# Softmax factors applied in the float16 split instead of in place, in an attention + two-layer kernel

## The chip, the cores and the metric

The kernel runs on one core of one Trainium2 chip. The metric is device time in microseconds (us) for one execution. Its engines are named as the profile names them: PE is TensorE (matrix products), PEld its weight loads, DVE is VectorE, ACT is ScalarE, POOL is GpSimd, and SP is SyncE, which here only issues DMAs. Each engine works through its own list of instructions in order, so an instruction that waits also holds up everything behind it on that engine.

## The reference

For 4 batches, 12 heads, 448 tokens and 64 numbers per head:

```
scores = cap * tanh((q @ k.T / sqrt(64)) / cap)          # cap = 30
p      = exp(scores - max(scores))
attn   = p / (sum(p) + 1e-9)
x      = heads of (attn @ v) side by side                # 1792 x 768
h      = x @ w_in                                        # 1792 x 2048
g      = max(h, 0) + alpha * min(h, 0)
out    = g @ w_out                                       # 1792 x 768, float32
```

## The kernel before

**Number format.** Most products run in float16 with float32 accuracy: an operand is split into a high part (its value rounded to float16) and a low part (the value minus the high part, again float16), and three products (high-high, high-low, low-high) are summed.

**Attention of batches 1 to 3.** The work is cut into 18 units (3 batches, 6 pairs of heads). A unit has 896 rows of scores (2 heads, 448 tokens), in 7 blocks of 128 rows and 448 keys; `steps` takes them two at a time. Per step: PE computes the scores into PSUM (L713), ACT writes their tanh into one of three buffers `tall` (L501), DVE takes each row's maximum (L506), POOL or DVE turns it into a bias (L508), ACT takes the exponential in place and sums each row (L513), DVE turns the sums into factors `rr`, which are 1/sum times 2^15 (L518, L520). Then, per block:

1. DVE multiplies the block in place by its factors (L522, recorded at L376, the line of the helper `scaled`).
2. ACT or DVE rounds it to float16: the high part, in one of three buffers `pw` (L536, recorded at L368 on ACT, L370 on DVE).
3. POOL or DVE subtracts: the low part (L537, recorded at L379, the helper `minus`).
4. SP issues one or two transposing DMAs from `pw` to `ptall` (L540), from which PE multiplies with the split `v` (L585); the result leaves PSUM by `xout` as another split pair, `xring`.

**Batch 0** works in float32 (`turn_32`: PE transposes the block, no split) except its last unit, of 4 blocks, which takes the way above with `gall` in the place of `tall`. So 126 + 4 = 130 blocks go through `turn_split`.

**The two layers.** `mm1` (L730) multiplies `xring` with `wi` and is evacuated by ACT or DVE (L374, L376), DVE (L740) and a split of `gr` into `gall` (high L368 or L370, low L379 on POOL or DVE). `mm2` (L771) multiplies `gall` with the split `w_out`. The weights arrive as 64-bit numbers and are converted and split by DVE, ACT and POOL (L826 to L841, L869 to L874). `mm1` of a batch needs all six units of its attention; `mm2` needs `mm1` of all its inner slices. While PE works on the attention of a batch, `mm1` and `mm2` of the batch before fill the rest of its time.

**The order** is written by a planner, `Plan`: each operation is given a priority and the engines that may do it with an expected time in ns, and a list scheduler gives the next ready operation to each free engine. Where an operation may go to ACT or DVE, its priority on DVE is worse by `PEN` = 114.44, and where to POOL or DVE, by `PEN2` = 133.12, so that DVE takes it only when it has little else ready. The expected times decide the order and the engine; the chip then runs the lists with semaphores.

Helpers that the change uses and that are there already:

```
scaled(e, o, i, s):      ACT: activation Copy with scale=s;  DVE: tensor_scalar o = i * s
split_lo(o, i, s, hi):   DVE: scalar_tensor_tensor o = (i * s) - hi
minus(e, o, a, b):       POOL or DVE: tensor_tensor o = a - b
```

`split_lo` is recorded at L382 and is used before for the splits of `q`, `k`, half of `v`, `xring` and part of the weights.

Of the kernel before, what the change touches and what calls it, by code (L numbers as in the profile page):

```python
# [75 lines left out]
class Plan:  # L76
# [15 lines left out]
    def op(self, prio, times, fn, r=(), w=(), rows=1.0):  # L92
        o = lambda: None
        o.prio, o.times, o.fn, o.rows, o.idx = prio, times, fn, rows, len(self.ops)
        o.handles, deps = [], set()
        for write, regions in ((False, r), (True, w)):
            for x in regions:
                if isinstance(x, Handle):
                    if x not in o.handles:
                        o.handles.append(x)  # L100
                        x.ops.append(o)
                    x = (x, 0, 1)
                space, lo, hi = x
                old = self.acc.setdefault(space, [])
                deps.update(e[2] for e in old if e[0] < hi and lo < e[1] and (write or e[3]))
                if write:
                    old[:] = [e for e in old if e[0] < lo or hi < e[1]]
        for write, regions in ((False, r), (True, w)):
            for x in regions:
                space, lo, hi = (x, 0, 1) if isinstance(x, Handle) else x  # L110
                self.acc[space].append((lo, hi, o.idx, write))
        o.deps = len(deps)
        o.next = []
        for d in deps:
            self.ops[d].next.append(o)
        self.ops.append(o)
        return o
# [114 lines left out]
def kernel(  # L232
# [89 lines left out]
    op = plan.op  # L322

    def chain(prio, fns, r=(), w=()):

        for fn in fns:
            op(prio, {"dve": 80}, lambda e, fn=fn: fn(), r=r, w=w)
# [38 lines left out]
    def copy(e, o, i):  # L366
        if e == "act":
            nc.scalar.activation(out=o, in_=i, func=AF.Copy)  # L368
        else:
            nc.vector.tensor_copy(o, i)  # L370

    def scaled(e, o, i, s):
        if e == "act":
            nc.scalar.activation(out=o, in_=i, func=AF.Copy, scale=s)  # L374
        else:
            nc.vector.tensor_scalar(out=o, in0=i, scalar1=s, scalar2=None, op0=ALU.mult)  # L376

    def minus(e, o, a, b):
        (nc.gpsimd if e == "pool" else nc.vector).tensor_tensor(out=o, in0=a, in1=b, op=ALU.subtract)  # L379

    def split_lo(o, i, s, hi):
        nc.vector.scalar_tensor_tensor(out=o, in0=i, scalar=s, in1=hi, op0=ALU.mult, op1=ALU.subtract)  # L382

    def either(n, psum=False):

        return {"act": 50 + 0.95 * n, "dve": 100 + (1.05 if psum else 0.55) * n}
# [63 lines left out]
    def spans(n, c):  # L450

        o = c * P
        for h in range(2):
            a, z = max(o, h * n), min(o + P, (h + 1) * n)
            if a < z:
                yield h, slice(a - o, z - o), slice(a - h * n, z - h * n)
# [11 lines left out]
    def t0_slot(i):  # L468

        if i % 5 < 4:  # L470
            a = i % 5 * 8
            lo = PART[1][0]
            return (gt[:, a:a + 8].rearrange("p (c j) k -> p c j k", j=NCH),
                    [(("g", r // 2), r % 2 * GW + lo, r % 2 * GW + lo + 2 * CP) for r in range(a, a + 8)])
        return pt32[:, -2 * S:].rearrange("p (c j k) -> p c j k", c=2, j=NCH), [("pt", 10 * S, 12 * S)]

    def steps(u, prio, n, S_, s_ns, sr_, scale, dma):

        nb = 2 * n // P
        u.sums = sums[:, u.idx % 3, :nb]  # L480
        for i0 in range(0, nb, 2):
            blocks = range(i0, min(i0 + 2, nb))
            m = len(blocks)
            i = step_no[0]
            step_no[0] += 1
            s = ps_s[i % 2]
            sr = (("S", i % 2), 0, 1)
            pr = prio + (ST1_P if u.b else ST_P) * i0

            def prods(e, blocks=blocks, s=s):  # L490
                for x, c in enumerate(blocks):
                    S_(s[:, x, :S], c)

            op(pr, {"pe": sum(s_ns(c) for c in blocks)}, prods, r=sr_, w=[sr])
            if u.b == 0:
                t, tr = t0_slot(i)
            else:
                t = tall[:, i % 3].rearrange("p c (j k) -> p c j k", j=NCH)
                tr = [("tall", i % 3 * 2 * S, (i % 3 + 1) * 2 * S)]
            t = t[:, :m]  # L500
            op(pr, {"act": 90 + 400 * m}, lambda e, s=s, t=t, m=m: nc.scalar.activation(  # L501
                out=t, in_=s[:, :m, :S].rearrange("p c (j k) -> p c j k", j=NCH), func=AF.Tanh, scale=scale[0]),
               r=[sr] + scale[1:], w=tr)
            mt = mxs[:, i % 6, :m]
            mr = (("m", i % 6), 0, 1)
            op(pr, {"dve": 20 + 490 * m}, lambda e, mt=mt, t=t: nc.vector.tensor_reduce(  # L506
                out=mt, in_=t, axis=AX.XY, op=ALU.max), r=tr, w=[mr])
            op(pr, {"dve": 130, "pool": 290}, lambda e, mt=mt: (nc.gpsimd if e == "pool" else nc.vector).tensor_scalar(  # L508
                out=mt, in0=mt, scalar1=ncap, scalar2=EXP_BIAS, op0=ALU.mult, op1=ALU.add), w=[mr])

            def exp(e, blocks=blocks, t=t, mt=mt):
                for x, c in enumerate(blocks):
                    nc.scalar.activation(out=t[:, x], in_=t[:, x], func=AF.Exp, scale=capt,  # L513
                                         bias=mt[:, x:x + 1], accum_out=u.sums[:, c:c + 1])

            op(pr, {"act": 735 * m}, exp, r=[mr], w=tr + [(("sums", u.idx % 3), c, c + 1) for c in blocks])
            r, rt = rr[:, u.idx % 3, i0:i0 + m], (("r", u.idx % 3), i0, i0 + m)
            chain(pr, (lambda r=r, su=u.sums[:, i0:i0 + m]: nc.vector.tensor_scalar(  # L518
                           out=r, in0=su, scalar1=GUARD, scalar2=1 / P_TOP if dma else 1.0, op0=ALU.add, op1=ALU.mult),
                       lambda r=r: nc.vector.reciprocal(out=r, in_=r)), r=[(("sums", u.idx % 3), i0, i0 + m)], w=[rt])  # L520
            for x, c in enumerate(blocks):
                op(pr, {"dve": 370}, lambda e, x=x, t=t, r=r: scaled(e, t[:, x], t[:, x], r[:, x:x + 1]), r=[rt], w=tr)  # L522
                if dma:
                    turn_split(u, pr, n, c, t[:, x], tr)
                else:
                    turn_32(u, pr, c, t[:, x], tr)

    blk_no = [0]

    def turn_split(u, pr, n, c, t, tr):  # L530

        w = pws[blk_no[0] % PW]
        wt = [(("pw", blk_no[0] % PW), z, z + 1) for z in range(2)]
        blk_no[0] += 1
        hi, lo = w[:, :NCH, :CP], w[:, NCH:, :CP]
        op(pr, {"act": 480, "dve": 310}, lambda e: copy(e, hi, t), r=tr, w=[wt[0]])  # L536
        op(pr, {"pool": 990, "dve": 540}, lambda e: minus(e, lo, t, hi), r=tr + [wt[0]], w=[wt[1]])  # L537
        for h, rows, cols in spans(n, c):
            full = rows.stop - rows.start == P
            op(pr, {"sp": (1294, 1275, 896) if full else (1225, 1275, 448)}, lambda e, h=h, rows=rows, cols=cols: nc.sync.dma_start_transpose(  # L540
                out=u.pt[h][:, :, cols], in_=w[rows].rearrange("p g k -> p (g k)")),
               r=wt, w=[("pt", u.po[h] + 4 * cols.start, u.po[h] + 4 * cols.stop)])

    def turn_32(u, pr, c, t, tr):

        h = plan.handle("a")

        def turn_P(e):
            for j in range(NCH):
                nc.tensor.transpose(ps_p[h.slot][:CP, j * P:(j + 1) * P], t[:, j], ident)  # L550

        ptw = ("pt", u.po[0] + c * P * NCH, u.po[0] + (c + 1) * P * NCH)
        op(pr, {"pe": 450}, turn_P, r=tr + [identr], w=[h, ptw])
        op(pr, either(512, True), lambda e: copy(
            e, u.pt[:, :, c * P:(c + 1) * P], ps_p[h.slot][:CP].rearrange("p (j t) -> p j t", j=NCH)), r=[h], w=[ptw])
# [64 lines left out]
    def attention32(part, pair):  # L620
# [30 lines left out]
        else:  # L651
            u.po = [po]
            u.pt = pt32[:CP, po:po + 8 * n].rearrange("p (j t) -> p j t", j=NCH)
        steps(u, prio, n, lambda s, c: nc.tensor.matmul(s, qz[:, c * P:(c + 1) * P], kt[:, pair], start=True, stop=True),  # L654
              lambda c: 750, [qr, ktr], [icap], dma)
        vt, vr = v0[0, pair]
# [371 lines left out]
```

## Time and profile before

| | |
|---|---|
| runs | 819.29, 820.54, 824.73 us; median 820.54 us |
| the profiled execution | 819.82 us; span from first to last instruction 818.0 us |
| PE | 712.3 us busy (87%), 4532 instructions |
| PEld | 419.5 us (51%) |
| DVE | 594.4 us (73%), 1250 instructions |
| ACT | 440.8 us (54%), 867 instructions |
| POOL | 313.1 us (38%), 307 instructions |
| mean granted TensorE clock | 0.949 |

Busy shares are averages over the whole span. The three stages differ: float32 attention and conversion of `w_in` up to about 160 us; attention of batch 1 with the conversion of `w_out` to about 300 us; attention of batches 1 to 3 beside `mm1` and `mm2` to about 660 us; then `mm2` and `mm1` alone.

### The profile page before, as it was taken

How to read it: one execution, taken by the hardware profiler on the slowest of the kernel's cores; microseconds unless marked ns; L12 is line 12 of the kernel's file. 1: busy time of each engine (PE TensorE's matmuls, PEld its weight loads, DVE VectorE, ACT ScalarE, POOL GpSimd, SP SyncE). 2: the span in 40 equal slices, each digit the busy share in tenths (PEclk: the TensorE clock that was granted, in tenths of full speed). 3: DMA queues.
4: the chain of work that ended last, by engine and by line, in shares of the span. 5: the costliest groups of instructions: out<-in, count | busy, mean ns of one | idle time of the engine just before them, and what ended most of it. 6: DMA issues, size and time to landing. Idle time of an engine off the chain costs nothing. (4 is left out here: it accounts for less than half of the span.)

```text
span 818.0 us, 12734 instructions
## 1 busy us (share of the span) xinstructions
PE 712.3 (87%) x4532; PEld 419.5 (51%) x4532; DVE 594.4 (73%) x1250; ACT 440.8 (54%) x867; POOL 313.1 (38%) x307
## 2 busy tenths in 40 slices
PE   8987877998678588947998998998899899999997
PEld 5655544676565244523444554554445455555664
DVE  3799997999999995797999976699889600344000
ACT  2767765887556673465765665476767400332000
POOL 1468563579675541333454522144454300000000
PEclk9999977999999599988999999999999999999999
DMA  9963422568646448877778867799876500000001
GB/s 212 274 202 119 156 77 89 164 119 169 164 133 129 90 80 165 157 171 152 126 128 152 152 129 162 138 192 161 161 147 114 100 20 20 20 1 1 20 20 38
DMA packets 227935, 98.62 MB, mean 121 GB/s; under 512 B 191456, under 2 KB 224160, under 8 KB 227872
## 3 DMA queue, kind: packets, MB, share of 16 engines
q1 hardware_dynamic: 227872, 97.82, 55.8%
q8 instruction: 35, 0.57, 0.3%
q14 instruction: 28, 0.23, 0.1%
HBM read 45.82 MB, written 5.51 MB: 63 GB/s over the span
## 5 line engine op out<-in xcount | busy, mean ns | idle before, releaser
L730 PE MATMUL p<-xring,wi 128*128 128x448 f16 (+2 forms) x1440 | 232.2, 320 | 8.9 <-DVE gr L740 8.0
L771 PE MATMUL p<-wp,gall 128*128 128x384 f16 x1344 | 230.2, 332 | 10.0 <-DVE gr L740 2.8
L730 PEld LDWEIGHTS <-wi 128*128 128x128 f16 x1440 | 138.0, 99 | 96.0 <-issue 14.5
L771 PEld LDWEIGHTS <-gall 128*128 128x128 f16 x1344 | 132.3, 99 | 102.6 <-issue 19.7
L379 POOL TENSOR_TENSOR pw<-tall,pw 128x448 f16<-128x448 f32 x100 | 115.6, 1160 | 118.0 <-ACT pw L368 66.4
L513 ACT ACTIVATE tall<-tall,mxs,small 128x448 f32<-128x448 f32 x126 | 94.4, 750 | 28.8 <-POOL mxs L508 21.4
L740 DVE SCALAR_TENSOR_TENSOR gr<-p,ca_g,gr 128x448 f32<-128x448 f32 (+2 forms) x80 | 46.4, 581 | 72.8 <-ACT gr L374 72.7
L368 ACT ACTIVATE pw<-tall 128x448 f16<-128x448 f32 x101 | 57.1, 572 | 66.7 <-DVE tall L376 45.5
L506 DVE TENSOR_REDUCE mxs<-tall 128x2 f32<-128x896 f32 x72 | 68.4, 958 | 13.5 <-ACT tall L501 13.2
L508 POOL TENSOR_SCALAR mxs<-mxs,small 128x2 f32<-128x2 f32 (+1 forms) x77 | 34.2, 444 | 112.4 <-DVE mxs L506 89.2
L501 ACT ACTIVATE tall<-s,ams 128x896 f32<-128x896 f32 x72 | 64.3, 903 | 21.5 <-PE s L713 19.6
L713 PE MATMUL s<-qkTs 128*128 128x448 f16 (+1 forms) x288 | 61.6, 377 | 15.4 <-DMA qkTs<-nat 14.2
L376 DVE TENSOR_SCALAR tall<-tall,rr 128x448 f32<-128x448 f32 x126 | 70.4, 567 | 0.5
L379 POOL TENSOR_TENSOR gall<-gr,gall 128x192 f16<-128x192 f32 (+4 forms) x56 | 49.0, 880 | 51.6 <-ACT gall L368 29.8
L374 ACT ACTIVATE wp<-p,small 128x384 f32<-128x384 f32 x21 | 12.1, 578 | 86.2 <-PE p L771 86.1
L585 PE MATMUL p<-ptall,vs 112*64 112x448 f16 (+1 forms) x456 | 49.2, 350 | 9.7 <-DMA ptall<-pw 8.3
L368 ACT ACTIVATE gall<-gr 128x384 f16<-128x384 f32 (+4 forms) x70 | 30.9, 445 | 43.0 <-DVE gr L740 42.8
L374 ACT ACTIVATE gr<-p,cs_g 128x448 f32<-128x448 f32 (+2 forms) x61 | 33.0, 540 | 37.5 <-PE p L730 36.8
L713 PEld LDWEIGHTS <-qkTs 128*128 128x128 f16 (+1 forms) x288 | 22.5, 103 | 42.9 <-DMA qkTs<-nat 17.7
L585 PEld LDWEIGHTS <-vs 112*64 112x64 f16 x456 | 27.4, 109 | 29.6 <-issue 14.7
L841 POOL TENSOR_TENSOR wi<-wi,wp 128x768 int32<-128x768 int32 x14 | 33.2, 2375 | 19.9 <-DVE wp L839 15.3
L654 PE MATMUL s<-tall,qkTs 128*128 128x448 f32 x84 | 40.3, 604 | 0.3 <-DVE qkTs L370 0.3
(149 smaller groups left out, 1008.7 us busy)
## 6 DMA issues: line engine op xcount, KB each, us to landing
wp<-in_moe_w_in_dram SPq DMA_DIRECT2D x16, 768.0 KB, 5.9
wp<-in_moe_w_out_dram SPq DMA_DIRECT2D x16, 768.0 KB, 4.5
rvs<-in_v_dram SPq DMA_DIRECT2D x38, 224.0 KB, 3.0
rqk<-in_q_dram SPq DMA_DIRECT2D x18, 224.0 KB, 3.0
rqk<-in_k_dram SPq DMA_DIRECT2D x18, 224.0 KB, 3.2
ptall<-pw SPq DMA_TRANSPOSE x148, 3.2
wp<-in_k_dram SPq DMA_DIRECT2D x6, 224.0 KB, 7.8
wp<-in_q_dram SPq DMA_DIRECT2D x6, 224.0 KB, 8.1
```

The lines of the kernel that those rows point to most:

```text
L368: nc.scalar.activation(out=o, in_=i, func=AF.Copy)
L374: nc.scalar.activation(out=o, in_=i, func=AF.Copy, scale=s)
L376: nc.vector.tensor_scalar(out=o, in0=i, scalar1=s, scalar2=None, op0=ALU.mult)
L379: (nc.gpsimd if e == "pool" else nc.vector).tensor_tensor(out=o, in0=a, in1=b, op=ALU.subtract)
L501: op(pr, {"act": 90 + 400 * m}, lambda e, s=s, t=t, m=m: nc.scalar.activation(out=t, in_=s[:, :m, :S].rearrange("p c (j k) -> p c j k", j= ...
L506: op(pr, {"dve": 20 + 490 * m}, lambda e, mt=mt, t=t: nc.vector.tensor_reduce(out=mt, in_=t, axis=AX.XY, op=ALU.max), r=tr, w=[mr])
L513: nc.scalar.activation(out=t[:, x], in_=t[:, x], func=AF.Exp, scale=capt, bias=mt[:, x:x + 1], accum_out=u.sums[:, c:c + 1])
L585: nc.tensor.matmul(pv[x * D:(x + 1) * D, :n], vs[:, z, c:c + D], u.pt[x][:CP, y * NCH + kc], start=(i == 0), stop=(i == len(prods) - 1))
L713: nc.tensor.matmul(s[rows], qT[:, x * S + cols.start:x * S + cols.stop], qkT[:, r0:r0 + NCH, :], start=(z == 0), stop=(z == 1))
L730: nc.tensor.matmul(ps_p[h.slot][:, :n], w[:, z, kk, :], x[:, d, o:o + n], start=(kk == 0 and z == d), stop=(kk == NPAIR - 1 and z == 1))
L740: op(pr, {"dve": 80 + 1.15 * n}, lambda e: nc.vector.scalar_tensor_tensor(out=t, in0=ps_p[h.slot][:, :n], scalar=ca_g[:, j:j + 1], in1=t, ...
L771: nc.tensor.matmul(ps_p[h.slot][:, :NH], g[j][:, d, t * P:(t + 1) * P], w[:, z, hf * NH:(hf + 1) * NH], start=(j == 0 and z == d), stop=(j ...
```

## The change

The multiplication in place is dropped where the split follows. The high part is now the block times its factor, rounded (ACT or DVE); the low part is the block times its factor, minus the high part, in one DVE instruction. POOL is no longer offered the low part. The float32 blocks of batch 0 keep the multiplication in place. The expected times of the two operations change with them.

```diff
             for x, c in enumerate(blocks):
-                op(pr, {"dve": 370}, lambda e, x=x, t=t, r=r: scaled(e, t[:, x], t[:, x], r[:, x:x + 1]), r=[rt], w=tr)
                 if dma:
-                    turn_split(u, pr, n, c, t[:, x], tr)
+                    turn_split(u, pr, n, c, t[:, x], tr, r[:, x:x + 1], rt)
                 else:
+                    op(pr, {"dve": 370}, lambda e, x=x, t=t, r=r: scaled(e, t[:, x], t[:, x], r[:, x:x + 1]), r=[rt], w=tr)
                     turn_32(u, pr, c, t[:, x], tr)
...
-    def turn_split(u, pr, n, c, t, tr):
+    def turn_split(u, pr, n, c, t, tr, f, fr):
...
-        op(pr, {"act": 480, "dve": 310}, lambda e: copy(e, hi, t), r=tr, w=[wt[0]])
-        op(pr, {"pool": 990, "dve": 540}, lambda e: minus(e, lo, t, hi), r=tr + [wt[0]], w=[wt[1]])
+        op(pr, {"act": 640, "dve": 470}, lambda e: scaled(e, hi, t, f), r=[*tr, fr], w=[wt[0]])
+        op(pr, {"dve": 680}, lambda e: split_lo(lo, t, f, hi), r=[*tr, fr, wt[0]], w=[wt[1]])
```

## Rows read from the trace of the kernel before

**Rows 1.** Busy time per stretch: start:end length, each engine's us (xinstructions), clock, DMA, GB/s.
```profile
160.00:300.00 140.00, 106.80 (x913) 78.52 (x912) 137.88 (x256) 92.81 (x191) 91.19 (x84) 0.90 0.61 131
300.00:660.00 360.00, 317.18 (x1889) 167.24 (x1887) 294.05 (x670) 217.79 (x432) 137.29 (x152) 0.97 0.75 144
660.00:818.00 158.00, 153.77 (x899) 87.76 (x897) 26.57 (x64) 26.63 (x46) 0.00 (x0) 0.99 0.07 18
```
**Rows 2.** Waits of PE, 300 to 660 us: us in total, times, longest.
```profile
PE p L355 <- DVE small L338: 12.1, 4, 8.3
...
PE p L585 <- DMA ptall<-pw: 8.3, 8, 2.2
```
**Rows 3.** Instructions on tile pw: ns minimum/median/maximum, first and last start.
```profile
L368 ACT ACTIVATE pw<-tall x101: 558/576/578, 183.4 to 648.3; 128x448 f16<-128x448 f32 x101
L379 POOL TENSOR_TENSOR pw<-tall,pw x100: 1025/1038/1744, 184.4 to 644.6; 128x448 f16<-128x448 f32 x100
L379 DVE TENSOR_TENSOR pw<-tall,pw x26: 604/625/1371, 216.8 to 648.9; 128x448 f16<-128x448 f32 x26
```
**Rows 4.** Groups of DVE, 160 to 300 us: busy us, mean ns, idle before.
```profile
L376 DVE TENSOR_SCALAR tall<-tall,rr 128x448 f32<-128x448 f32 x22 | 15.9, 726 | 0.0
...
L506 DVE TENSOR_REDUCE mxs<-tall 128x2 f32<-128x896 f32 x11 | 11.7, 1072 | 0.2 <-ACT tall L501 0.2
...
L382 DVE SCALAR_TENSOR_TENSOR nat<-rqk,ams,nat 112x512 f16<-112x512 f32 x6 | 7.7, 1293 | 0.0
```
**Rows 5.** The same view, 300 to 660 us.
```profile
L376 DVE TENSOR_SCALAR tall<-tall,rr 128x448 f32<-128x448 f32 x104 | 54.5, 533 | 0.5
L506 DVE TENSOR_REDUCE mxs<-tall 128x2 f32<-128x896 f32 x43 | 45.8, 1077 | 13.0 <-ACT tall L501 12.8
L382 DVE SCALAR_TENSOR_TENSOR nat<-rqk,ams,nat 112x512 f16<-112x512 f32 x28 | 24.9, 901 | 0.5 <-ACT nat L374 0.5
...
L379 DVE TENSOR_TENSOR pw<-tall,pw 128x448 f16<-128x448 f32 x25 | 16.6, 666 | 9.4 <-ACT pw L368 7.8 <-issue 1.2
L370 DVE CAST pw<-tall 128x448 f16<-128x448 f32 x24 | 10.6, 444 | 5.7 <-DMA ptall<-pw 5.0 <-POOL mxs L508 0.5
```
**Rows 6.** Instructions of lines L376, L382, L379: ns minimum/median/maximum, whole span.
```profile
L376 DVE TENSOR_SCALAR tall<-tall,rr x126: 431/444/2018, 171.0 to 644.0; 128x448 f32<-128x448 f32 x126
...
L376 DVE TENSOR_SCALAR nat<-rqk,ams x16: 469/483/1268, 123.5 to 612.7; 112x512 f16<-112x512 f32 x16
...
L382 DVE SCALAR_TENSOR_TENSOR nat<-rqk,ams,nat x36: 729/744/2273, 124.8 to 614.6; 112x512 f16<-112x512 f32 x36
...
L382 DVE SCALAR_TENSOR_TENSOR vs<-rvs,vam,vs x9: 720/739/1539, 204.1 to 616.5; 112x512 f16<-112x512 f32 x9
...
L379 DVE TENSOR_TENSOR vs<-rvs,vs x3: 673/678/1393, 365.4 to 452.3; 112x512 f16<-112x512 f32 x3
```
**Rows 7.** Groups of ACT by shape, whole span: with a factor per row, and without.
```profile
L374 ACT ACTIVATE nat<-rqk,ams 112x512 f16<-112x512 f32 x20 | 14.0, 710 | 1.5 <-DVE ams L335 1.5
...
L368 ACT ACTIVATE vs<-rvs 112x512 f16<-112x512 f32 x9 | 5.5, 616 | 0.0
```
**Rows 8.** Busy time per stretch on tile pw alone: DVE, ACT, POOL.
```profile
160.00:300.00 140.00, 2.13 (x3) 13.17 (x23) 28.27 (x24) 0.90 0.61 131
300.00:660.00 360.00, 27.12 (x49) 45.69 (x81) 91.84 (x80) 0.97 0.75 144
```
**Rows 9.** Waits of ACT and DVE, 160 to 660 us: us in total, times, longest.
```profile
ACT pw L368 <- DVE tall L376: 45.5, 41, 2.8
...
DVE pw L379 <- ACT pw L368: 7.8, 5, 4.8
...
DVE nat L382 <- ACT nat L374: 0.5, 2, 0.3
```
**Rows 10.** Timeline at 359 us: start, us, engine, line, operation; an instruction beside a POOL subtraction.
```profile
358.95 2.04 POOL L379 TENSOR_TENSOR pw<-tall,pw 128x448 f16<-128x448 f32 x2 [2.07 <-ACT pw L368]
359.02 1.00 DVE L333 TENSOR_SCALAR ams<-ams 128x2 int32<-128x2 int32 x1
```

## The prediction

> **What bounds the kernel now.** I read the busy times by stretch first, since the shares of the whole span mix stages [rows 1]. From 660 us on, PE has 153.8 of 158 us and nothing of the change runs there: that part stays. From 160 to 300 us DVE is busy 137.9 of 140 us while PE has 106.8: DVE sets the pace, and a us of DVE saved is a us of time. From 300 to 660 us PE has 317.2 of 360 and DVE 294.1: neither is full, PE is nearer. PE's 42.8 idle us are the most that this stage can give back. PE's work is fixed, so the question is what PE waits for: the view of waits names, among others, the maxima of the next `q` and `k` on DVE (12.1 us, once for 8.3) and the landing of the transposed blocks (8.3 us) [rows 2]. Both are ends of chains in which the changed steps stand or beside which they are queued.
>
> The second thing to see is how unsteady DVE's instructions are. The multiplication in place has a median of 444 ns and a maximum of 2018 [rows 6]; its mean is 726 ns in the first stage and 533 in the second [rows 4, 5]. The row maximum L506 has 1072 and 1077, no spread at all [rows 4, 5]. The timeline shows one such case: a POOL subtraction begins at 358.95, and an instruction of two columns that DVE starts at 359.02 takes 1.00 us, until the first of two subtractions is over [rows 10]. So some DVE instructions stand still while POOL works. POOL's work on `pw` is 28.3 of its 91.2 us in the first stage (0.31) and 91.8 of 137.3 in the second (0.67) [rows 1, 8]. All of it goes.
>
> **The change, part by part.** 130 blocks: 22 + 4 in the first stage (the 4 of batch 0's last unit priced like the 22), 104 in the second.
>
> *Low part on DVE, a form that the trace lacks at this size.* Lower end: the plain subtraction on the same operands, 625 ns [rows 3]. Upper end: the same operation on 512 columns, 744 [rows 6]. On 512 columns the fused form has 739 and the plain one 678 [rows 6], 61 more, so I take 625 + 61 = 686 ns, between the ends.
>
> *High part.* On ACT a factor per row costs 710 - 616 = 94 ns [rows 7]: 576 [rows 3] becomes 670 (ends 576 and 710). On DVE, between the cast's mean of 444 [rows 5] and 483 for a scaled one of 512 columns [rows 6]: 450. I leave the shares of the engines as they are, 26 on DVE.
>
> *DVE, own work.* First stage: out go 26 x 0.726 = 18.9 us and 2.1 us of `pw` [rows 4, 8], 21.0; in come 26 x 0.686 + 2 x 0.45 = 18.7. Second: out go 104 x 0.533 + 25 x 0.666 + 24 x 0.444 = 82.7 [rows 5]; in come 104 x 0.686 + 24 x 0.45 = 82.1. Without stalls the added work equals the removed.
>
> *Stalls of the new low parts by the POOL work that stays.* The multiplication lost 0.726 - 0.444 = 0.28 us each in the first stage and 0.09 in the second; with 0.69 and 0.33 of POOL's work left, 0.195 x 26 + 0.03 x 104 = 8.2 us. The nearer operation, the subtraction with two inputs on DVE, lost only 0.666 - 0.625 = 0.04 in the second stage [rows 3, 5], which with 0.33 makes 1.4 us in place of 3.1. I take 5.1 and 3.1, the dearer; with 1.4 the second stage would be 1.7 us better. The Trainium skill ("SBUF — State Buffer", section "Who interferes with whom") says that a VectorE instruction with two SBUF inputs contends with a GpSimd instruction that reads SBUF, the loser being blocked for the other's whole length. By that rule the low part is no safer than the multiplication was, which speaks for the 8.2; the subtraction's 1371 ns maximum [rows 3] agrees.
>
> *Relief of other DVE work.* Lower end: the split of `q` and `k` alone lost 6 x (1.293 - 0.744) = 3.3 us in the first stage and 28 x (0.901 - 0.744) = 4.4 in the second [rows 4 to 6]; times 0.31 and 0.67, 1.0 and 2.9 us. Upper end: each of the other 227 and 517 DVE instructions [rows 1, 8] loses what the multiplication lost, 0.28 x 0.31 x 227 = 20 and 0.09 x 0.67 x 517 = 31 us. Reductions, and whatever reads PSUM, show no spread, so well below the middle: 7 and 12 us.
>
> DVE's net is then -2.3 + 5.1 - 7 = -4 us in the first stage and -0.6 + 3.1 - 12 = -9.5 in the second.
>
> *What reaches the end.* First stage: 4 us, one for one. Second: PE is the fuller engine and covers part; I take half, 5 us. *Chain of a block:* before 0.444 + 0.576 + 1.038 = 2.06 us from factor to DMA, after 0.670 + 0.686 = 1.36. PE's 8.3 us of waiting for `ptall` can shrink by at most that; I take 3 us, with what POOL, now free, takes over of the other low parts of `gr`. Lower bound for both is nothing.
>
> *What I cost at nothing.* ACT's 104 x 0.094 = 9.8 us: ACT has 310.6 of 500 us busy [rows 1], and the high part no longer waits for the multiplication, which held ACT 45.5 us [rows 9]. If that cover fails they delay tanh and exponentials of the next step by up to 9.8 us. SP's transposes wait for the low part as before, now for DVE instead of POOL; queued behind them are the loads and the transposes of `q` and `k`. The three `pw` buffers are held 0.670 + 0.686 instead of 0.576 + 1.038 before the DMA, so 0.26 us less; they give no new wait. The planner counts DVE as dearer than before (680 against 370 per block, while 26 subtractions of 540 go), so it will hand more choices to ACT and POOL.
>
> Sum: 4 + 5 + 3 = 12 us off the profiled execution's 819.8, 808 us. The median of the runs is 820.5, so the same 808 stands for it.
>
> **The rivals.**
>
> *A, PE covers it.* The stage after 300 us is PE's and DVE's saving falls into DVE's idle 66 us; only the first stage gives its 4 us: 816. For it: PE's 317 of 360. Against it: PE does wait there, for DVE chains by name [rows 2]. If the planner's new order leaves DVE the work that POOL could take, it ends here too.
>
> *B, DVE waits for ACT.* Before, POOL did the waiting for the high part; now DVE, in order, stands in front of it, and behind it are row maxima, factors and evacuations. The 25 low parts that DVE had in the second stage brought 9.4 us of idle time, 0.38 each [rows 5]. At that price 25 more in the first stage cost 9.5 us at once, and 79 more in the second 30 us, half of which DVE's idle time takes: 9.5 + 15 = 24.5 us over the forecast, 832. It cancels the gain from 12 / (25 + 79/2) = 0.19 us per low part. Against it: the same pair, ACT high and DVE low, for `q` and `k` waits 0.5 us in total [rows 9], and DVE took those 25 because it had nothing better to do.
>
> *C, the stalls were most of the trouble.* Relief near the upper ends, 15 us in the first stage in place of 7, and 12 of the second stage's 42.8 us of PE idle instead of 5 + 3: 12 + 12 = 24 off, 796.
>
> *D, the change does not do what it says:* the planner gives high parts to DVE on a large scale. 24 more of them cost DVE 11 us, 104 cost 47; the penalty of DVE and the dearer DVE times speak against it. It counts with B.
>
> **How the numbers follow.** Forecast 0.46 (802 to 813), A 0.24 (813 to 823), B with D 0.20 (826 to 840), C 0.10 (785 to 799). A measurement of this kernel tells about 1% from no change, that is 812.3 and 828.7. Faster: nearly all of the forecast, 0.40, and C, 0.10. Same: A, 0.24, and the rest of the forecast, 0.06. Slower: B, 0.20. The range leaves out the dearer half of B and the better half of C: 790 to 832.
>
> **What would show it.** L376 on `tall` is gone and POOL has no `pw`, so POOL's busy time falls by some 120 us. L382 on `pw` stands 130 times on DVE with a median near 686 ns; ACT's `pw` near 670. The mean of the split of `q` and `k` falls from 901 ns towards 744 in the second stage. DVE's wait for ACT's `pw` stays under some 10 us in all; at 25 or more, B is right. PE's idle time between 300 and 660 us falls by less than DVE's busy time. I am wrong if DVE's busy time does not fall at all, or if PE's idle time stays and DVE's falls.

## The result and the profile after

The changed kernel takes 784.02 us (783.89 to 786.47), the kernel before in the same comparison 820.28: a ratio of 0.9555, 95% interval 0.9515 to 0.9594, so 36 us or 4.5% faster. I forecast 808, with a range from 790 to 832. The profiled execution has 784.08 us, its span 782.3.

Busy time per engine, from the page of the changed kernel:

```profile
PE 704.1 (90%) x4532; PEld 415.2 (53%) x4532; DVE 563.7 (72%) x1200; ACT 451.8 (58%) x877; POOL 207.3 (27%) x217
```

DVE fell by 30.7 us (594.4 before) and POOL by 105.8. PE's idle time, span less busy, fell from 818.0 - 712.3 = 105.7 to 782.3 - 704.1 = 78.2 us. That is 27.5 of the span's 35.7; the other 8.2 are PE's busy time, with the same 4532 products.

The same stretches as in [rows 1] (the last ends with the span):

```profile
160.00:300.00 140.00, 114.97 (x960) 83.47 (x961) 135.32 (x266) 103.13 (x207) 64.32 (x59) 0.91 0.62 136
300.00:660.00 360.00, 337.29 (x2046) 179.64 (x2044) 263.78 (x608) 220.58 (x428) 58.28 (x86) 0.98 0.77 144
660.00:783.00 123.00, 117.99 (x680) 66.22 (x678) 26.59 (x64) 23.72 (x41) 0.00 (x0) 1.00 0.06 17
```

PE does 8 us more in the first of these stretches (106.80 before) and 20 us more in the second (317.18 before), so less is left for the end: 118.0 us in the last one, 153.8 before. The waits of PE from 300 to 660 us, answering [rows 2]:

```profile
PE s L713 <- DMA qkTs<-nat: 14.5, 8, 7.2
PE p L355 <- DVE small L338: 3.8, 4, 2.4
...
PE p L585 <- DMA ptall<-pw: 0.2, 1, 0.2
```

Both waits that I named have shrunk, from 12.1 and 8.3 us to 3.8 and 0.2. The largest that is left, for the transposed `q` and `k` (L713), has grown: it was 10.2 us before. The new instructions on `pw`, minimum/median/maximum, answering [rows 3]:

```profile
L382 DVE SCALAR_TENSOR_TENSOR pw<-tall,rr,pw x126: 658/676/2053, 174.7 to 637.4; 128x448 f16<-128x448 f32 x126
L374 ACT ACTIVATE pw<-tall,rr x95: 651/660/671, 172.5 to 636.7; 128x448 f16<-128x448 f32 x95
L376 DVE TENSOR_SCALAR pw<-tall,rr x31: 431/453/1156, 238.1 to 633.4; 128x448 f16<-128x448 f32 x31
```

And the groups of DVE from 300 to 660 us, answering [rows 5] (busy us, mean ns, idle before):

```profile
L382 DVE SCALAR_TENSOR_TENSOR pw<-tall,rr,pw 128x448 f16<-128x448 f32 x102 | 69.1, 692 | 12.5 <-ACT pw L374 12.1 <-ACT tall L501 0.2
...
L382 DVE SCALAR_TENSOR_TENSOR nat<-rqk,ams,nat 112x512 f16<-112x512 f32 x26 | 18.8, 743 | 0.0
```

The split of `q` and `k` now has a mean of 743 ns in this stretch (901 before), which is its undisturbed median of 744 [rows 6]: its stalls are gone in this stretch. Before 300 us some remain: over the whole span the mean is 797 ns.

### The profile page after: what moved, and what is told of

Its sections match the earlier page's. It is cut to its first block, busy times and chain, and to the rows that moved or that the text cites. A ratio compares the mean times of both kernels' runs of the same rounds, so it can differ in the third digit from the quotient of the medians.

```text
span 782.3 us, 12555 instructions
## 1 busy us (share of the span) xinstructions
PE 704.1 (90%) x4532; PEld 415.2 (53%) x4532; DVE 563.7 (72%) x1200; ACT 451.8 (58%) x877; POOL 207.3 (27%) x217
## 5 line engine op out<-in xcount | busy, mean ns | idle before, releaser
L730 PE MATMUL p<-xring,wi 128*128 128x448 f16 (+2 forms) x1440 | 229.8, 319 | 3.6 <-POOL wi L379 2.5
L771 PE MATMUL p<-wp,gall 128*128 128x384 f16 x1344 | 227.9, 330 | 4.4 <-POOL wp L379 2.0
L382 DVE SCALAR_TENSOR_TENSOR pw<-tall,rr,pw 128x448 f16<-128x448 f32 x126 | 91.2, 737 | 12.5 <-ACT pw L374 12.1
L508 POOL TENSOR_SCALAR mxs<-mxs,small 128x2 f32<-128x2 f32 (+1 forms) x85 | 37.8, 444 | 229.0 <-DVE mxs L506 183.2
L379 POOL TENSOR_TENSOR gall<-gr,gall 128x192 f16<-128x192 f32 (+4 forms) x62 | 58.5, 947 | 115.5 <-ACT gall L368 73.8
L374 ACT ACTIVATE pw<-tall,rr 128x448 f16<-128x448 f32 x95 | 61.8, 661 | 38.4 <-DMA ptall<-pw 25.4
L713 PE MATMUL s<-qkTs 128*128 128x448 f16 (+1 forms) x288 | 63.2, 384 | 19.3 <-DMA qkTs<-nat 18.5
L501 ACT ACTIVATE tall<-s,ams 128x896 f32<-128x896 f32 (+1 forms) x72 | 64.2, 904 | 24.5 <-PE s L713 22.8
L374 ACT ACTIVATE gr<-p,cs_g 128x448 f32<-128x448 f32 (+2 forms) x66 | 35.4, 537 | 46.8 <-PE p L730 44.9
L368 ACT ACTIVATE gall<-gr 128x384 f16<-128x384 f32 (+4 forms) x76 | 32.9, 438 | 40.4 <-DVE gr L740 40.4
L713 PEld LDWEIGHTS <-qkTs 128*128 128x128 f16 (+1 forms) x288 | 22.8, 105 | 49.0 <-DMA qkTs<-nat 22.3
L841 POOL TENSOR_TENSOR wi<-wi,wp 128x768 int32<-128x768 int32 x14 | 33.2, 2377 | 20.1 <-DVE wp L839 15.5
L585 PEld LDWEIGHTS <-vs 112*64 112x64 f16 x456 | 26.0, 111 | 22.7 <-issue 7.6
L841 POOL TENSOR_TENSOR wp<-wp,wp 128x768 int32<-128x768 int32 x14 | 27.7, 1981 | 22.5 <-DVE wp L839 8.6
```

The costliest lines, as they stand in the source:

```text
L585: nc.tensor.matmul(pv[x * D:(x + 1) * D, :n], vs[:, z, c:c + D], u.pt[x][:CP, y * NCH + kc], start=(i == 0), stop=(i == len(prods) - 1))
L713: nc.tensor.matmul(s[rows], qT[:, x * S + cols.start:x * S + cols.stop], qkT[:, r0:r0 + NCH, :], start=(z == 0), stop=(z == 1))
L730: nc.tensor.matmul(ps_p[h.slot][:, :n], w[:, z, kk, :], x[:, d, o:o + n], start=(kk == 0 and z == d), stop=(kk == NPAIR - 1 and z == 1))
L771: nc.tensor.matmul(ps_p[h.slot][:, :NH], g[j][:, d, t * P:(t + 1) * P], w[:, z, hf * NH:(hf + 1) * NH], start=(j == 0 and z == d), stop=(j ...
L841: op(prio, {"pool": 1760}, lambda e: nc.gpsimd.tensor_tensor(out=f, in0=f, in1=lo, op=ALU.add), r=[sr], w=[fr])
```

## The experiments

Twelve further kernels; each is compared with the kernel before on the same chip. Three theories to begin with: S, POOL's subtractions stall DVE; C, the chain from factor to DMA is shorter; O, the planner wrote a better order. Later K: the plan has to know that the low part is DVE's; and L: orders scatter by chance. H, W and Q are named where they are tested.

| kernel | median us | ratio to before | 95% interval |
|---|---|---|---|
| the change | 784.02 | 0.9555 | 0.9515 to 0.9594 |
| its instructions, order of before | 808.5 | 0.9868 | 0.9803 to 0.9934 |
| instructions of before, its order | 824.79 | 1.0067 | 1.0039 to 1.0095 |
| POOL's subtraction again | 828.71 | 1.0112 | 1.0070 to 1.0154 |
| before, low parts on DVE only | 811.55 | 0.9920 | 0.9892 to 0.9948 |
| plan with a multiplication | 784.97 | 0.9572 | 0.9506 to 0.9637 |
| low part planned on POOL | 806.6 | 0.9839 | 0.9763 to 0.9915 |
| shorter times in the plan | 796.37 | 0.9703 | 0.9641 to 0.9766 |
| longer times in the plan | 789.57 | 0.9591 | 0.9495 to 0.9688 |
| POOL reads constants | 829.19 | 1.0080 | 1.0048 to 1.0112 |
| POOL writes only | 787.64 | 0.9579 | 0.9534 to 0.9625 |
| direct splits of v and w_in | 790.2 | 0.9624 | 0.9572 to 0.9675 |
| weights without POOL | 771.99 | 0.9390 | 0.9341 to 0.9439 |

**The changed instructions in the order of before.** The three planned operations of before stay; what they issue is changed.

```diff
-op(pr, {"dve": 370}, ... scaled(e, t[:, x], t[:, x], r[:, x:x + 1]) ...)
+op(pr, {"dve": 370}, ... None if dma else scaled(e, t[:, x], t[:, x], r[:, x:x + 1]) ...)
-op(pr, {"act": 480, "dve": 310}, lambda e: copy(e, hi, t), ...)
-op(pr, {"pool": 990, "dve": 540}, lambda e: minus(e, lo, t, hi), ...)
+op(pr, {"act": 480, "dve": 310}, lambda e: scaled(e, hi, t, f), ...)
+op(pr, {"pool": 990, "dve": 540}, lambda e: split_lo(lo, t, f, hi), ...)
```

> The changed kernel's instructions in the order that the planner writes for the kernel before: the planner is still told of a multiplication on DVE (370 ns), a high part (480/310) and a low part on POOL or DVE (990/540), but the multiplication issues nothing, the high part is scaled, and the low part is always DVE's fused one. Theory S (POOL's subtractions stalled DVE; some 40 us of stalls on DVE between 160 and 650 us are gone): 784 to 795 us, and DVE's means at their medians. Theory C (the shorter chain from factor to DMA): the same, 784 to 795. Theory O (the new order of the planner does it): 812 to 822, little changed from before.

808.5 us: the instructions alone give 12 us of the 36; the interval of the ratio allows 5 to 16. All three theories missed. This kernel has both the shorter chain and no subtraction of POOL on `pw`, so in this order S and C together do not give the gain; O, by which the instructions do next to nothing, gives too little. DVE's busy time, from its page, is already down by 24 us:

```profile
PE 709.8 (88%) x4532; PEld 419.7 (52%) x4532; DVE 570.3 (71%) x1224; ACT 447.4 (56%) x867; POOL 197.4 (25%) x203
```

PE's idle time is 805.1 - 709.8 = 95.3 us, and the two waits of PE from 300 to 660 us are nearly those of before:

```profile
PE p L355 <- DVE small L338: 13.7, 7, 8.0
...
PE p L585 <- DMA ptall<-pw: 6.8, 8, 2.3
```

Its stretches, to be set beside those of [rows 1]:

```profile
160.00:300.00 140.00, 112.66 (x950) 82.54 (x948) 136.88 (x265) 97.12 (x195) 66.08 (x61) 0.90 0.61 132
300.00:660.00 360.00, 322.25 (x1937) 171.63 (x1936) 271.34 (x636) 221.57 (x430) 46.85 (x71) 0.98 0.76 145
```

**The instructions of before in the changed order.**

```diff
-... lambda e: scaled(e, hi, t, f) ...
+... lambda e: (scaled("dve", t, t, f), copy(e, hi, t)) ...
-... lambda e: split_lo(lo, t, f, hi) ...
+... lambda e: minus("pool", lo, t, hi) ...
```

> The instructions of the kernel before (multiplication in place on DVE, rounding, subtraction, the last now on POOL for all 130 blocks) in the order that the planner writes for the changed kernel. S and C: 815 to 835 us, DVE's stalls back. O: 784 to 795.

824.79 us: the new order with the old instructions is worth nothing, as S and C had it. But this order was planned without a multiplication and with the low part on DVE, so it is a wrong plan for these instructions, and the run does not tell what a good order would be worth to them. Instructions and order are worth more together than apart.

**POOL's subtraction again.** A scratch is written that nothing reads.

```diff
-... lambda e: split_lo(lo, t, f, hi) ...
+... lambda e: (split_lo(lo, t, f, hi), minus("pool", idle, t, hi)) ...
```

> The changed kernel with POOL's 130 subtractions issued again beside it, from the same operands into a scratch that nothing reads (POOL about 135 us busier, no result depends on it). S: most of the gain is lost, 800 to 815 us, with the means of the split of q and k and of L333 on DVE up again. C: the chain to the DMA is as short as in the changed kernel, so 784 to 790. O: 784 to 790.

828.71 us. More than the whole gain is lost, though the chain to the DMA has the same two steps as in the changed kernel. That is in the direction of S, whose own range ended at 815, and against C as the main cause. The low part itself became slower, though, 977 ns in the mean against 737, so the chain takes longer than in the changed kernel; and the scratch also held `t` and `pw` longer, which the constants below take up.

**Before, with low parts on DVE only.**

```diff
-op(pr, {"pool": 990, "dve": 540}, lambda e: minus(e, lo, t, hi), ...)
+op(pr, {"dve": 540}, lambda e: minus(e, lo, t, hi), ...)
```

> The kernel before with one part of the change alone: the low part is offered to DVE only (540 ns), the multiplication in place stays. DVE gets 104 x 0.625 = 65 us more work of its own. S: about 40 us of stalls go, so DVE is about 25 us worse off: 825 to 845 us. C: the chain falls from 2.06 to 1.65 us per block, over half of the way: 800 to 812. O says nothing here.

811.55 us: S missed by 13 us at least, and the time lies in C's range. Whether it does so for C's reason this run cannot tell, since it takes away POOL's reads and changes the order too; no run shortened the chain alone. I had added 65 us of own work on DVE and taken off 40 of stalls. Its page shows DVE hardly busier:

```profile
PE 709.8 (88%) x4532; PEld 419.2 (52%) x4532; DVE 601.6 (74%) x1312; ACT 454.9 (56%) x895; POOL 217.6 (27%) x217
```

That is 7.2 us above before. 104 more low parts came to DVE, but its instructions rose only from 1250 to 1312: the planner had moved 42 other choices off DVE, since it knew that DVE was loaded and POOL free. That led to K and to the next four.

**A multiplication in the plan.** As the first experiment, but the planner is given the changed times.

```diff
-op(pr, {"act": 480, "dve": 310}, lambda e: scaled(e, hi, t, f), ...)
-op(pr, {"pool": 990, "dve": 540}, lambda e: split_lo(lo, t, f, hi), ...)
+op(pr, {"act": 640, "dve": 470}, lambda e: scaled(e, hi, t, f), ...)
+op(pr, {"dve": 680}, lambda e: split_lo(lo, t, f, hi), ...)
```

> The changed kernel's instructions; the planner is told the changed times (640/470, and 680 on DVE alone) and, in front of each block, of a multiplication of 370 ns on DVE that issues nothing. After the first four runs: the instructions alone in the old order gave 12 us, the new order with the old instructions nothing, both together 36. Theory K (the plan has to know that the low part is DVE's and POOL is free): 784 to 792 us. Theory H (the plan has to know that the path from factor to DMA is short, so that PE and SP find their work earlier in their lists): 797 to 810. Theory L (orders scatter by chance, by 10 us and more): anywhere.

**The low part planned on POOL.** The changed kernel with one line of the plan as before.

```diff
-op(pr, {"dve": 680}, lambda e: split_lo(lo, t, f, hi), ...)
+op(pr, {"pool": 990, "dve": 540}, lambda e: split_lo(lo, t, f, hi), ...)
```

> The changed kernel's instructions, no multiplication in the plan, but the planner is told that the low part goes to POOL in 990 ns or to DVE in 540; it is issued on DVE either way. K: 797 to 812 us, DVE overloaded against its plan. H: 784 to 795, since the planned path is short. L: anywhere.

784.97 and 806.6 us. With the first experiment and the change these make a square, all four issuing the same operations per block (the upper left also has the old expected times for the high part):

| | low part planned on POOL or DVE | on DVE |
|---|---|---|
| multiplication in the plan | 808.5 | 784.97 |
| none | 806.6 | 784.02 |

The multiplication in the plan costs 1 or 2 us, so theory H is out. Where the plan puts the low part is worth 22 to 24 us in both rows, and both new corners lie in K's ranges. The plan that puts it on DVE also leaves DVE fewer instructions, 1224 to 1182 in the upper row and 1255 to 1200 in the lower, the rest having gone to ACT and POOL; DVE's busy time is 6.2 and 10.2 us lower for it. PE's wait for `ptall` in the two new corners, 300 to 660 us; first with the multiplication in the plan and the low part on DVE:

```profile
PE p L585 <- DMA ptall<-pw: 0.4, 1, 0.4
```

and with the low part planned on POOL:

```profile
PE p L585 <- DMA ptall<-pw: 5.9, 6, 1.9
```

Within the square PE waits for `ptall` in both orders that think the low part is POOL's (6.8 and 5.9 us) and hardly in the others (0.4 and 0.2). My reading is that in the first two DVE does low parts that the plan had given to POOL, and so reaches later items later than PE's list expects. That is argued, not shown, and the wait is no sure sign of it: with the shorter times below it is back, though the low part is planned on DVE,

```profile
PE p L585 <- DMA ptall<-pw: 8.8, 5, 2.2
```

and in the fastest kernel of all, the last experiment, it is 14.3 us. Which displaced items make up the 23 us was not separated.

**Shorter, and longer, times in the plan.**

```diff
-{"act": 640, "dve": 470} ... {"dve": 680}
+{"act": 575, "dve": 375} ... {"dve": 600}
```

> The changed kernel with smaller expected times in the plan for the same instructions: high part 575/375, low part 600 (from the trace's 660, 453 and 676 ns less the overlap with the next instruction). K and H: within 1% of the changed kernel, 778 to 792 us. L: as likely above 795 as below.

```diff
-{"act": 640, "dve": 470} ... {"dve": 680}
+{"act": 700, "dve": 520} ... {"dve": 740}
```

> The same the other way: high part 700/520, low part 740 in the plan. K and H: 778 to 792 us. L: as likely above 795 as below; both of this pair near 784 would speak against L.

796.37 and 789.57 us. The shorter times fell outside the 778 to 792 that K allowed: orders scatter by some 12 us with times that are all defensible, so L has a part. The four orders that plan the low part on DVE lie at 784 to 796, the two that plan it on POOL at 807 and 808.5, and they do not mix. But these are six orders, and the gap between the groups, 10 us, is no wider than the scatter within the first. K is the best account of the 23 us; that chance has a share in them is not excluded.

**POOL reads constants.** Stalls without held buffers.

```diff
+    nc.gpsimd.memset(idle, 0.0)
+    nc.gpsimd.memset(still, 0.0)
...
-... lambda e: split_lo(lo, t, f, hi) ...
+... lambda e: (split_lo(lo, t, f, hi), minus("pool", idle, still, idle)) ...
```

> The changed kernel with 130 extra subtractions on POOL, of the size of the removed ones, from two buffers of zeros into one of them: they wait for nothing and hold no buffer of the attention; no result depends on them. With the block's own operands the extra subtractions took all of the gain and more (829 us). Theory S (POOL's reads stall DVE): 812 to 830 us, DVE's stalls back. Theory W (it was the holding of tall and pw until POOL was done): 784 to 795.

**POOL writes only.**

```diff
+... lambda e: (split_lo(lo, t, f, hi), nc.gpsimd.memset(still, 0.0), nc.gpsimd.memset(still, 0.0)) ...
```

> The changed kernel with two memsets of 448 numbers on POOL per block (about 0.9 us) in the place of that subtraction: POOL as busy, but it reads nothing; no result depends on it. S: the fused low part no longer stalls, only instructions of one input do, so less than half of e5's loss: 788 to 803. Theory Q (the small bias of the maxima and the other low parts queue behind POOL's extra work): as slow as e5.

829.19 and 787.64 us. W and Q are out: with nothing held the loss is the same as with the block's operands, and with POOL nearly as busy (330.8 us against 369.1) but reading nothing it is 4 us, just under the range that S gave. The added work on POOL and the two kinds of DVE instruction, with constants read (lines are shifted by two; columns as above):

```profile
L381 POOL TENSOR_TENSOR idle<-still,idle 128x448 f16<-128x448 f32 x130 | 161.2, 1240 | 7.3
...
L384 DVE SCALAR_TENSOR_TENSOR pw<-tall,rr,pw 128x448 f16<-128x448 f32 x126 | 110.1, 886 | 4.1 <-ACT pw L376 4.0
L384 DVE SCALAR_TENSOR_TENSOR nat<-rqk,ams,nat 112x512 f16<-112x512 f32 x36 | 32.9, 931 | 0.1
L378 DVE TENSOR_SCALAR pw<-tall,rr 128x448 f16<-128x448 f32 x31 | 22.1, 719 | 1.3 <-DMA ptall<-pw 1.0
```

and with memsets (shifted by one):

```profile
L538 POOL MEMSET still<- 128x448 f32 x260 | 127.3, 490 | 12.7
...
L383 DVE SCALAR_TENSOR_TENSOR pw<-tall,rr,pw 128x448 f16<-128x448 f32 x126 | 90.5, 731 | 12.1 <-ACT pw L375 11.8
L383 DVE SCALAR_TENSOR_TENSOR nat<-rqk,ams,nat 112x512 f16<-112x512 f32 x36 | 28.3, 805 | 0.1
L377 DVE TENSOR_SCALAR pw<-tall,rr 128x448 f16<-128x448 f32 x31 | 16.5, 536 | 3.0 <-DMA ptall<-pw 2.8
```

In the changed kernel the three means over the whole span are 737, 797 and 487 ns. The subtraction of constants lengthens all three; the one that read the block's own operands lengthened the first two, to 977 and 1071, and left the third at 472, at the same loss of time; the memset leaves the two operations with two SBUF inputs where they were and lengthens only the one with one input, a little. The Trainium skill ("SBUF — State Buffer", section "Who interferes with whom") says that an instruction with two SBUF inputs contends with a GpSimd instruction that reads SBUF, not with one that only writes. The runs agree with it: 886 and 931 ns beside the reads, 731 and 805 beside the memsets. That sentence does not speak of the operation with one input, which grew beside the constants and the memsets, to 719 and 536 ns.

**Direct splits of v and w_in.**

```diff
-VA = 0.5
-AI = 0
+VA = 1.0
+AI = 1.0
```

> The changed kernel and the same step at two more places: all splits of v and of w_in go directly (factor in the high part, fused low part on DVE, nothing on POOL). DVE gets 16 low parts of w_in at about 1.0 us before 160 us, where it is full, and loses the 13 us of stalls that the trace shows beside POOL's subtractions of w_in. Forecast 776 to 792, likeliest no change.

**And weights without POOL.**

```diff
-XI = 0
-XO = 0.25
-AO = 0.75
+XI = 1.0
+XO = 1.0
+AO = 1.0
```

> That, and the conversion and the split of all weights without POOL: the fused conversion on DVE (1.1 us in place of 0.55 on DVE and 2 on POOL, 24 chunks) and direct splits of w_out. DVE +13 us of own work for the conversions and -20 us of stalls. If stalls are the price of POOL's work in general, 765 to 782; if DVE's own work decides before 300 us, 785 to 800.

790.2 us, as forecast no gain: it is 6 us slower than the changed kernel, within the scatter of orders. And 771.99 us, inside the 765 to 782 forecast for the case that stalls are the price of POOL's work, which beats both kernels. The page of the second:

```profile
PE 695.7 (90%) x4518; PEld 413.4 (54%) x4518; DVE 534.8 (69%) x1212; ACT 440.0 (57%) x863; POOL 112.1 (15%) x162
```

POOL has lost 95 us more against the changed kernel and DVE, which took over the conversions, is not busier but 28.9 us less so. The scatter of orders is as large as these 12 us, so how much of them the missing work of POOL gives is open.

## Why the prediction was wrong

**The step that failed** stands under "What I cost at nothing": "The planner counts DVE as dearer than before (680 against 370 per block, while 26 subtractions of 540 go), so it will hand more choices to ACT and POOL." I saw the direction and gave it no time of its own. It is the largest term: 23 us, measured twice in the square, some of which may be the chance of orders. The direction was right, 42 and 55 instructions left DVE there; but they lowered its busy time by only 6 and 10 us. The rest must lie in where the operations stand in the lists, and which of them matter stays open. Rival A even had the new order with the opposite sign.

**The sum of the instructions came out for the order that I reasoned in, in part by luck.** With the order of before kept, the change gives 820.3 - 808.5 = 12 us (5 to 16 by the interval), the 12 that I forecast. The prices of the new instructions were right: the low part at 676 ns against 686, the high part at 660 and 453 against 670 and 450. The savings on DVE were not: 1.0 us in the first stage against my 4, and 22.7 in the second against 9.5. In the second stage the new steps cost 82.9 us where the old had cost 82.7, so nearly all of the 22.7 is relief of other work (a few instructions had also moved ahead of 300 us), where I had 12. I had let the share of POOL's work that goes, 0.67, stand for the share of the stalls, while the split of `q` and `k` fell from 901 to 768 ns in this run, most of the way to 744. Nor did the gain come where I put it: PE did 5.9 and 5.1 us more work in the two stages, where I had 4 and 8. One sentence of mine misleads: "Without stalls the added work equals the removed" compares added work without stalls with removed work that includes them.

**What reaches the end** was judged with PE's list as it was. In the new order PE's waits for the chains that I named fell by 16 us together [rows 2], and its idle time there by 20, not by the 8 I took for this stage. "PE's work is fixed" did not hold in time: the same 4532 products took 8.2 us less. PE's mean granted clock in the two profiles was 0.949 and 0.954; how much of the 8.2 us that makes no run separates.

**Rival B did not come.** DVE waited 12.1 us for ACT's high parts in all, 0.12 each over 102 in the second stage, not 0.38; below the 0.19 at which it would have cancelled the gain. **Rival C** had the sign and the mechanism, stalls, but the instructions alone do not give its 24 us. In the new order such stalls are dear: 130 subtractions on POOL cost 829.2 - 784.0 = 45 us. That is not the price of what the change took away, since the kernel before had 104 of them on POOL, the others on DVE, and an order planned for them.

**What I expected to see** was mostly seen: POOL's fall (105.8 us for some 120, since it took over other work), the medians, the split of `q` and `k` at 744, and from 300 to 660 us PE's idle time falling by less than DVE's busy time, 20.1 against 30.3. DVE's wait for ACT's `pw` was a little over the 10 us that I allowed.

## What to carry to other kernels

Before pricing a move between engines, ask who writes the order: where a planner does, keep its list and change the instructions, then tell it the truth, and take the two results apart. GpSimd work that reads SBUF can have a second price, paid by VectorE: compare an instruction's median and mean, and look for the difference again in what runs beside it. Two or three orders from slightly different expected times show how much of a gain may be chance; here it was 12 us of scatter beside an effect of 36.

## What the runs showed of the hardware

A GpSimd memset of 128 x 448 float32 numbers took 490 ns, and 260 of them left the fused VectorE instructions at a mean of 731 ns (737 without); 130 GpSimd subtractions at 1240 ns raised the same instructions to 886. That reading, and not being busy, is what cost these instructions their time was not visible in the traces of before and after.
